# A one-tile first block, Q and K from the unpacked weights, single-row weight loads and five early gate tiles in a fused attention and gMLP kernel

## The chip, the cores and the metric

The kernel runs on one core of a Trainium2 chip. The metric is the device time of one execution in microseconds (us). Before the change it is 280.43 us, the median of three runs (279.98 to 282.6).

## The reference

One block of 2048 tokens with 448 features passes two layers, each with a residual. The first is attention with 16 heads of 28 features over a sliding window of 256 tokens, the second a gMLP: a spatial gating unit whose mixing matrix `w_sp` works over the tokens. A vector `c` gives shift, scale and gate of both.

```python
mod = (_silu(c) @ w_mod).reshape(c.shape[0], 6, 1, -1)
sa, ca, ga, sb, cb, gb = (mod[:, i] for i in range(6))
h = _layernorm(x) * (1 + ca) + sa
x = x + ga * _A_ref(h, A_wqkv, A_wo)
h = _layernorm(x) * (1 + cb) + sb
x = x + gb * _B_ref(h, B_w_in, B_w_sp, B_b_sp, B_w_out)

def _A_ref(x, wqkv, wo):          # H = 16, Dh = 28, W = 256
    q, k, v = split(x @ wqkv)
    scores = q @ k.T * Dh ** -0.5             # 0 <= i - j < W
    return softmax(scores) @ v @ wo

def _B_ref(x, w_in, w_sp, b_sp, w_out):       # Fh = 896
    z = gelu(x @ w_in)
    z1, z2 = z[..., :Fh], _layernorm(z[..., Fh:])
    return (z1 * (w_sp @ z2 + b_sp[:, None])) @ w_out
```

All inputs and the output are bfloat16.

## The kernel before

**Engines and queues.** The tokens are cut into 16 tiles of 128. PE (TensorE) does all matrix products, ACT the exponentials, gelus and some evictions from PSUM, DVE statistics, normalisations and most evictions, POOL the masks, the root of the layer norms and some elementwise work, and SP issues the DMAs (ACT issues two). Every operation is an entry that `P.op` creates, numbered from 0 in the order in which the program creates it. The string `ORDER` lists all entries once. An item such as `125.2/4` is entry 125, done by the third of its possible engines, with slot 4 of its buffer pool. The entries of one engine are emitted in the order of the string, and each engine works its own queue strictly in that order; semaphores make it wait for what other engines deliver. Where entries of different engines stand to each other in the string therefore says nothing; what stands ahead of what on one engine says all.

**The ramp.** SP loads the tokens (`load_x`), two of the six column groups of `w_mod` (`wmodA`, in two halves, the second of them issued by ACT), and the weights of Q, K, V (`wqk_raw`, `wv_sb`). PE runs 44 filler products of 256 columns on zeros (`warm`) and four groups of 16 small ones (`warmt`) between its real work. `c` goes to columns by four one-row products (`c_cols`), ACT takes their silu (`silu0` loads the table, `silu` computes, `exp0` loads the table of the exponential). `modA`, 32 one-column products, gives shift and scale, and two DVE operations evict them (`modAe0`, `modAe1`).

**Blocks.** Tokens are normalised and projected in blocks of 2, 2, 2, 2, 4, 4 tiles (`blocks`). For the first four, `transp_pe` transposes by PE and an eviction to `hT` applies shift and scale; for the last two SP transposes by DMA. The 448 features are held as four chunks of 128 rows, the third of which has 64 rows twice (`CH = (0, 128, 192, 320)`): weights are loaded with these rows doubled, and the doubled half is zeroed (`zv`, `zqk`) or left out. Eight operations (`wqkp`) copy Q and K weights from `wqk_raw` to `WQK`, where each head has 32 columns. `project` runs eight chains of four products per block for Q and K (`qk`), evicted to `QKT` (`qke`), and one chain per tile for V (`v`, evicted by `ve`).

**Attention.** For tile j there are up to three key tiles. `S` is one block of 16 score products, four at a time on strips of 32 rows; two exponentials `E` of 128x1024 follow on ACT, a mask `M` on POOL where needed, and two groups `PV` of eight value products. 90 exponentials are run in all. Then come the division, a DMA transpose (`oT`), the output projection (`wo`), the residual (`x1`), the second layer norm (`l2`, `x2`), a DMA transpose (`h2T`) and shift and scale (`h2m`).

**gMLP.** The gate half `z2` of tile t is seven steps of 448 columns on PE (`z2m`; six full ones and one in which two half-height products run side by side). For ordinary tiles ACT takes the gelu straight from PSUM, which needs a change of the ACT table and so waits for the last exponential. For the raw tiles (`zraw`, tiles 0 and 1) DVE or ACT copies the product to `z2` in SBUF (`z2e`), and ACT takes the gelu from there later. `z1m` and `z1s` give the other half, transposed, in steps of 512 columns. SP transposes `w_sp` in 32 pieces (`wsp`). `G` is 28 groups of 16 products of 512 columns (in quarters), `out` the last product, and `fin` adds the residual.

Of the kernel before, what the change touches and what calls it, by code (L numbers as in the profile page):

```python
# [4 lines left out]
ACT = mybir.ActivationFunctionType  # L5
# [159 lines left out]
0 16 7 1 21 20 17 18 26 23 28 27 118 120 2 3 1673/0 1674 1675 1676 1677 1678 1679 1680 1681 1682 1683 1684 1685 29/2 1686 1687 1688 1689 1690 1691  # L165
1692 1693 1694 25 30 1695 32/1 33 34 31 8 9 14 6 10 5 4 12 15 13 11 50 119 51 121 54 52 122 53 19 22 55 123 24 56 58/0 124 57 125.2/4 126.2/1 35 1696
1697 1698 1699 1700 36 37 1701 60/0 38 1702 1703 39 59/3 127/0 131/2 40 41 49 46 45 48 47.1 128 61 62.1 63.1 65/1 1704 64 1705 1706 132 1707 1708 1709
66 67 134 129.1 130.1 42 43 44 323 319 321 325 324 326 320 322 327 93/3 88/7 98/0 89 90 103/2 104 99 100 101 91 94 83/1 105 68/6 69 106 70 84 102 92
107 133 85 71 78/7 86 79 95 96 80 81 87.1 72 97 73/0 74 82 75 76 113/6 114 115 116 252 185 77 487/0,1 488/3 491/6 328 329 330.1/1 117.1 333.1/4
332.1/3 489 492 331.1/2 1710 108/4 109 110 1711 140/1 111 141 142 1712 1713 143 145/0 146 147 1714 1715 1716 148 502/1,0 112 155/2 156 157 158 186 254  # L170
253 255 187 402 188 189 404 159.1 403 256 144 149 485/1 135/0 136 1717 137 138 1718 165/2 166 167 168 506/0 503/1 486 509/0,1 139 169 493/0 490 170/2
171 1719 1720 172 180/1 181 182 183 173 160/3 161 162 163 510/7 512/9 184 522/0,1 150/1 151 152 153 494 495/1 257 258 507 504 190 408 406 174.1 191
334 336 337 496/1 335 154.1 505/0 513 511 508 407 514 515/2 405 164 526/10 523/3 529/1,2 530/7 192.1/3 193.1/0 259.1/4 175/1 176 177 178 179.1 516/0
533/1 194/0 195 409 196 197 536/0,1 198/1 199 200.1 201.1 222/3 497/2 498 499 500 207/0 223 208 209 210 224 202/1 203 225 539/4 537/5 211 226 549/0,1
553/8 550/6 260.1/1 531 410 501 932 265/2 204 205 206.1 212/3 232/0 213 214 215 233 266 234 235 216.1 517/1 518 519 520 227/3 521 534 524 411 412 554
527 413.1/3 415.1/0 236 268 267 556/1,0 560/0 557/9 228 229 230 538/0 237/2 217/1 525 238 239 231.1 934 218 219 262/3 261 220 240 532 535 340 241.1
221 264.1 263.1 563/1,0 540 528 564/2 566/4 269/1 242/3 314/2 243 270 315 316 317 244 245 576/1,0 541 933 935 542/2 318.1 936 246.1 577/5 580/3 294/0
295 271 272 296 247/2 297 279/3 248 249 280 281 250 273.1 274/1 275 276 282 277 419 543/1 903 900 902 901 298.1 283.1 278.1 251 583/1,0 284/0 299/2
300 301 302 285 286 287 584/7 587/10 303.1 289/1 290 291 292 288.1 590/1,2 591/1 416.1/2 561 558 414.1/1 551 418 339.1 937 341.1 567/0 555 552 938
293.1 939/2 581 578 941/0 588 585 338.1 559 565 562 593/6 603/1,0 544/1 545 546 547 607/8 604/4 568 569/2 548 917/0 918 919 920 921 922 610/2,0 611/9  # L180
923 924 614/2 925 926 309/1 310 311 312 313.1 579/0 589 617/1,2 594 304/1 305 306 586 307 592 582 947 308.1 420 417 612 423.1 605 615 940 570/1 595
596/1 948 906 618/10 620/0 630/1,0 634/5 631/3 347/1 348 349 352/3 571/2 353 354 355 342/0 350 572 637/0,1 573 574 356.1 421 575 351 638/1 641/6 343
344 345 357/1 358 346.1 644/0,2 359 360 621/0 613 616 606 619 645/7 647/2 657/1,0 661/9 658/4 949 950 361.1 951 362/1 635 608 609 622 623/2 632 942
944.1 952 642 953 956.1/2 954.1/1 422.1 639 662 363 387/2 364 388 389 392/3 393 365 372/0 394 366 664/1,0 668/0 665/10 373 390 391.1 669 367/1 368 369
374 370 371.1 395 396.1 424 375 1410 904 1409 597/3 907 598/2 599 1408 624/2 909 943.1 659 957 955 960.1 666 671/0,1 376 674/8 600 601 636/0 377/1 378
379 648 602 672/5 684/1,2 380 685/2 633 640 646 643 688/7 381.1 691/1,0 625/1 626 627 628 649 650/2 629 397/0 398 399 400 401.1 692/1 695/6 698/2,1
382/1 383 384 385 699/3 908 910 905 651/0 911 912 673/0 701/5 660 675 711/0,2 715/4 712/8 386.1 962 964 663 670 667 963 676 677/1 430/1 431 432 433
718/1,2 652/0 653 654 655 434.1 965 966 656 977 978 450/1 451 719/9 722/10 686 693 945.1 689 696 961.1 713 723 716 958.1 720 725/1,0 678/3 914 913
1415 1414 452 714/0 728/0 435/3 436 437 438 729 460/2 453 461 726/8 454 738/1,0 742/0 727 721 739/8 717 724 425/1 426 427 428 462 463 429 745/1,0 967
439.1 968 971/1 969/0 740 730 731/2 749/9 746/10 694/0 690 679/1 680 681 682 464.1 683 979 980 981 982 743 747 750 702 752/2,0 755/4 697 455/1 456 457  # L190
458 687 753/5 765/1,0 700 459.1 703 704/0 445/1 446 447 448 769/1 766/7 772/2,0 773/3 776/6 946.1 732/1 733/0 734 735 736 970 972 1412 1411 705/0 1413
449.1 737 959 983 994 440/1 441 442 779/2,1 782/2 756/0 744 748 741 443 751 780/4 444.1 792/0,1 754 757 758/1 465/1 466 467 468 796/10 799/1,2 793/8
469.1 995 470/0 471 472 473 800/0 986/0 767 777 984/1 770 774 474.1 803/9 480/1 481 482 483 806/0,1 775/0 778 781 771 783 768 484.1 784 785/2 807/5
809/4 819/2,0 823/3 475/1 476 477 478 804 801 794 797 973.1 479.1 987 976 974 808/0 802 798 820/6 826/0,1 810 795 805 830/1 824 821 831 827/2 759/1
915 985 916 828 760/1 761 762 763 811 812/1 833/1,2 764 1007 1008 836/9 825/0 832 927/1 834/5 846/0,2 847/4 850/0 822 837 835 829 853/1,0 929 838
839/0 857/3 854/8 786/3 813/2 1419 1416 840/1 1417 706/3 707 814/2 708 815 816 709 990.1 991.1 988.1 817 860/0,1 975.1 848 858 851 989.1 855 931 930
928 710 818 992 993 996 863/1 861/10 852/0 787/1 788 789 790 849 873/2,1 859 864 856 862 791 997 998 865 866/2 874/2 877/9 875 880/0,2 841/1 842 843
# [22 lines left out]
1585/3 1597/1 1598 1586 1443 1629 1638 1444 1445/1 1446 1568 1455 1456 1570 1621/1 1622 1457/1 1458 1483/3 1541/0 1623 1484 1624 1542 1495/5 1625/1  # L220
1485/0 1496 1487/4 1488 1630 1489/2 1571 1490 1486 1497/3 1615/5 1626 1498 1572 1631/2 1632 1552 1616 1573/0 1617 1574 1618 1619/2 1543/1 1611/6
1599/2 1620 1600 1612 1601/0 1602 1544 1665/5 1666 1657/3 1667/3 1613/2 1668 1658 1669/4 1614 1607/1 1670 1608 1671/0 1659/3 1661/6 1609/2 1603/7 1672
1610 1662 1604 1660 1553/3 1663/0 1554 1664 1491/0 1555/1 1492 1605/2 1556 1606 1493/3 1494
"""

PARAMS = {
# [857 lines left out]
```

## Time and profile before

| quantity | us |
|---|---|
| median of three runs (lowest, highest) | 280.43 (279.98, 282.6) |
| span of the profiled execution, first to last instruction | 279.1 |
| DVE busy in the span | 156.1 |
| ACT busy; of this in 90 exponentials | 135.4; 84.4 |
| POOL busy | 94.2 |
| first modulation product on PE | 8.00 |
| first projection on PE | 11.85 |
| first scores on PE, first exponential on ACT | 17.32, 17.77 |
| last scores on PE | 109.89 |
| granted TensorE clock | 1.000 |

The profile is one execution. A line of the order of time has the start, the time, the engine (PEld is the weight load of PE, ACTq and SPq the DMA queues), the line of the program, the operation, what it writes and reads, how many instructions were merged into it, and in brackets how long the engine had been idle and what ended that. All PE instructions have line 435, so they are told apart by what they write and read. Matmul ends are modelled and overlap the next start, so work is best read from start to start.

### The profile page before, as it was taken

Reading aid. Unit: us, or ns where it says so; the run is one execution under the profiler, and the core shown is the slowest. Engines: PE = TensorE matmul, PEld = TensorE weight load, DVE = VectorE, ACT = ScalarE, POOL = GpSimd, SP = SyncE. Lnnn points to the kernel's source line nnn. Section 1 sums busy time; section 2 is a strip of 40 time slices with the busy share of each in tenths; the row PEclk is TensorE's granted clock in tenths of the full one; section 3 lists DMA queues with packets and bytes.
Section 4 is the critical chain, followed back from the end, with each engine's and each line's share of the span. In section 5 each row is a group of like instructions: output and inputs, shape, how many; then the busy total and the mean of one; then the engine's idle time right before and its main releaser. Section 6 shows DMA issues by size and latency. Waiting matters only on the chain.

```text
span 279.1 us, 6498 instructions
## 1 busy us (share of the span) xinstructions
PE 268.0 (96%) x2750; PEld 142.8 (51%) x2776; DVE 156.1 (56%) x373; ACT 135.4 (49%) x183; POOL 94.2 (34%) x156
## 2 busy tenths in 40 slices
PE   8899999999999988999999999999999999999995
PEld 4667677655565645444344444444444444444452
DVE  5688775576757688597385841332424230433543
ACT  4689999999999999866566600000000000000000
POOL 4166796755568677646322120000000000000000
PEclk9999999999999999999999999999999999999999
DMA  7954129796587683469999700000000000000223
GB/s 240 366 125 76 23 42 203 131 168 161 145 152 133 126 154 77 94 113 169 172 167 189 133 4 0 0 2 0 0 0 0 19 0 0 2 0 0 66 79 105
DMA packets 67503, 25.38 MB, mean 91 GB/s; under 512 B 56337, under 2 KB 67346, under 8 KB 67474
## 3 DMA queue, kind: packets, MB, share of 16 engines
q1 hardware_dynamic: 67200, 24.50, 42.5%
q8 instruction: 22, 0.36, 0.6%
q10 hardware_dynamic: 274, 0.46, 0.5%
q14 instruction: 7, 0.06, 0.1%
HBM read 9.48 MB, written 1.84 MB: 41 GB/s over the span
## 4 chain that ended last, share of the span: by engine, by line
PE 79%; ACT 16%; DMA 2%; issue 1%; DVE 1%; SPq 0%
PE ps L435 79%; ACT PT L796 13%; DMA wmod_sb<-in_w_mod_dram 2%; ACT hT L622 2%; ACT QKT L718 1%; SPq L466 0%; DVE fin L1005 0%; DVE x_sb L842 0%; DVE st_all L543 0%; ACT Vaug L729 0%
## 5 line engine op out<-in xcount | busy, mean ns | idle before, releaser
L796 ACT ACTIVATE PT<-ps 128x1024 bf16<-128x1024 f32 x90 | 84.4, 1078 | 2.6 <-PE ps L435 2.3
L986 DVE TENSOR_TENSOR tmpg<-ps,bsp_bc 128x512 bf16<-128x512 f32 x28 | 19.3, 691 | 59.2 <-PE ps L435 59.2
L435 PE MATMUL ps<-QKT,z 128*128 128x512 bf16 x219 | 50.7, 379 | 0.3
L804 POOL TENSOR_SCALAR_AFFINE_SELECT PT<-PT 128x512 f32<-128x512 f32 x60 | 37.2, 638 | 11.3 <-ACT PT L796 11.3
L435 PE MATMUL ps<-hT,WQK 128*128 128x256 bf16 (+1 forms) x182 | 34.6, 305 | 2.2 <-ACT hT L622 0.8
L435 PEld LDWEIGHTS ps<-QKT,z 128*128 128x128 bf16 x224 | 21.9, 98 | 26.4
L551 POOL TENSOR_TENSOR rs_all<-ve_all,neghalf 128x1 f32<-128x1 f32 (+2 forms) x31 | 20.0, 650 | 38.1 <-DVE ve_all L550 37.8
L435 PE MATMUL ps<-w_in_sb,hT 128*128 128x448 bf16 (+1 forms) x128 | 29.2, 353 | 0.1
L435 PE MATMUL ps<-hT,w_in_sb 128*128 128x512 bf16 (+1 forms) x106 | 27.5, 379 | 0.5 <-DVE st_all L543 0.3
L435 PE MATMUL ps<-w_spC,z 128*128 128x512 bf16 x110 | 26.7, 379 | 0.1
L435 PE MATMUL ps<-w_spD,z 128*128 128x512 bf16 x109 | 26.1, 379 | 0.2
L435 PEld LDWEIGHTS ps<-Vaug,PT 128*128 128x128 bf16 x720 | 22.7, 97 | 5.8 <-ACT PT L796 0.4
L435 PE MATMUL ps<-Vaug,PT 128*128 128x29 bf16 x720 | 25.0, 176 | 0.5 <-POOL PT L804 0.2
L543 DVE BATCH_NORM_STATS2 st_all<-z2raw 128x6 f32<-128x448 bf16 x32 | 18.6, 615 | 10.4 <-ACT z2raw L899 10.3
L435 PEld LDWEIGHTS ps<-hT,WQK 128*128 128x128 bf16 x192 | 16.9, 97 | 10.8 <-ACT hT L622 1.8
L435 PE MATMUL ps<-w_out_sb,z1T 128*128 128x448 bf16 x112 | 22.3, 352 | 0.0
L633 POOL TENSOR_SCALAR hT<-hT,modT 128x256 bf16<-128x256 bf16 (+1 forms) x31 | 18.5, 601 | 10.8 <-DMA hT<-xn 10.8
L564 POOL TENSOR_SCALAR xn<-x_sb,rs_all,nm_all 128x512 bf16<-128x512 bf16 x23 | 17.5, 769 | 8.0 <-DVE nm_all L555 4.3
L543 DVE BATCH_NORM_STATS2 st_all<-x_sb 128x6 f32<-128x448 bf16 x32 | 18.9, 615 | 1.7 <-DMA x_sb<-in_A_x_dram 1.5
L435 PE MATMUL ps<-QKT 28*128 28x128 bf16 x720 | 18.1, 217 | 1.7 <-ACT PT L796 1.3
L721 DVE CAST QKT<-ps 128x256 bf16<-128x256 f32 (+1 forms) x27 | 14.2, 531 | 8.3 <-PE ps L435 7.9
L918 ACT ACTIVATE z1T<-ps 128x512 bf16<-128x512 f32 x28 | 15.6, 600 | 5.8 <-PE ps L435 5.7
(70 smaller groups left out, 273.3 us busy)
## 6 DMA issues: line engine op xcount, KB each, us to landing
wmod_sb<-in_w_mod_dram SPq DMA_DIRECT2D x8, 224.0 KB, 4.0
w_in_sb<-in_B_w_in_dram SPq DMA_DIRECT2D x8, 224.0 KB, 3.8
out_dram<-fin SPq DMA_DIRECT2D x16, 112.0 KB, 1.7
x_sb<-in_A_x_dram SPq DMA_DIRECT2D x3, 448.0 KB, 8.3
wqk_raw<-in_A_wqkv_dram SPq DMA_DIRECT2D x2, 452.0 KB, 7.3
bsp_bc<-in_B_b_sp_dram SPq DMA_DIRECT2D x1, 512.0 KB, 5.8
x_sb<-in_A_x_dram SPq DMA_DIRECT2D x2, 224.0 KB, 3.3
wmod_sb<-in_w_mod_dram ACTq DMA_DIRECT2D x1, 448.0 KB, 4.5
```

Of the source, the lines that this page charges most:

```text
L435: return e.matmul(out_, lhsT=lhsT, rhs=rhs, start=st, stop=sp, **kw)
L543: st = [dve("%sst%d" % (name, i), prio, dve_ns(D), lambda e, i=i, s_=s_: e.bn_stats(st_all[:, slot, t, i, :], s_()), deps, tens) for i, s_ ...
L551: r = pool(name + "rs", prio, 420 + 148 * n, lambda e: e.tensor_tensor(rs_all[:, slot, t0:t1], ve_all[:, slot, t0:t1], neghalf[:, t0:t1], ...
L564: return e.tensor_scalar(dst, src, rs_all[:, slot, t:t + 1], nm_all[:, slot, t:t + 1], ALU.mult, ALU.add)
L622: return e.activation(hT[:, c_, cols], ps[:, ten.slot, q * 256:q * 256 + 256], ACT.Identity, bias=modT[:, c_:c_ + 1], scale=modT[:, 4 + c_ ...
L633: return e.tensor_scalar(hT[:, c_, cols], hT[:, c_, cols], modT[:, base_col + 4 + c_:base_col + 5 + c_], modT[:, base_col + c_:base_col + ...
L718: return e.activation(QKT[:, g, cols], ps[:, ten.slot, 0:w], ACT.Copy)
L721: return e.tensor_copy(QKT[:, g, cols], ps[:, ten.slot, 0:w])
L796: e_op = P.op("E%d_%d" % (j, ui), pr, [("act", 925, lambda e, ten=ten, pt=pt: e.activation(PT[:, pt.slot, :, :], ps[:, ten.slot:ten.slot + ...
L804: ready = pool("M%d_%d" % (j, ui), pr - 50, pool_ns(512), lambda e, pt=pt, pat=pat, cm=cm, cmp=cmp: e.affine_select(out=pt32(pt.slot), in_ ...
L918: g = P.op("z1g%d_%d" % (tb, ft), pr - 19, [("act", act_ns(512), lambda e: e.activation(z1T[:, ft, tb * 512:(tb + 1) * 512], ps[:, ten.slo ...
L986: a = dve("ga%d_%d" % (tb, ft), pr, dve_ns(512), lambda e, tb=tb, ten=ten, tg=tg: e.tensor_tensor(tmpg[:, tg.slot, :], ps[:, ten.slot, :], ...
```

## The change

- `blocks` becomes 1, 1, 2, 2, 2, 4, 4. `transp_pe` has four PSUM banks for the first block and two for the others, and one entry evicts all chunks of a bank.
- The features are held as four chunks of 112 rows. All weight loads become `load_112`, two DMAs of 224 rows; nothing is doubled, and `zv`, `zqk`, `zc`, `cz0` and `cz1` go. wmodA has 16 columns more, wmodG 16 fewer. A memset `xpad` zeroes the pad of `xn`.
- For block 0 Q and K are computed from `wqk_raw`: a step is four products with 32 weight columns each, on four column strips. `WQK` is still packed for the other blocks.
- The scores of tile 0 are two entries of eight products, one for each pair of head groups.
- `zraw` covers tiles 0 to 4. Ordering rules that kept z1, z2, gelus and G behind the last scores or the last exponential are removed from the list of entries.
- `ORDER` is new as a whole. Read per engine, its queues begin, or stand around the end of attention, as follows.

| queue | before | after |
|---|---|---|
| ACT, start | c, wmodA1, silu0, silu, exp0, xn2, xn3 | c, silu0, silu, exp0, wmodA1, xn1 |
| PE, fillers ahead of c_cols | 12 warm, 1 warmt | 19 warm, 3 warmt |
| PE, fillers between modA and the first tr, then up to the first qk | mixed with modA and tr | 5, then 5 behind tr |
| PE, ahead of the first scores | qk of block 0, v of tile 1 | qk of block 0, 28 steps of qk of block 1, two tr of block 2 |
| PE, z steps ahead of the last scores | none | 35 of z2 (tiles 0 to 4), 6 of z1 |
| PE, wo of tiles 14, 15 and last PV | first z steps among them | further back among the z steps |
| SP, w_sp transposes behind the oT of tile 13 | 22 | 28 |

```diff
-    'blocks': (2, 2, 2, 2, 4, 4),
+    'blocks': (1, 1, 2, 2, 2, 4, 4),
+    'raw': (1, 0, 0, 0, 0, 0, 0),
-    'zraw': (0, 1),
+    'zraw': tuple(range(5)),
...
+    def load_112(name, prio, dst, w, a, b, order=(), o=0, engs=("sp", "sp"), rate=292.0):
         return [load("%s%d" % (name, h), prio + 0.001 * h,
-                     lambda e, h=h: e.dma_start(dst[:, 2 * h:2 * h + 2, a - o:b - o], w[192 * h:192 * h + 256, a:b].rearrange("(c p) n -> p c n", p=128)),
-                     256 * (b - a) * 2, order=order, eng=engs[h], rate=rate) for h in range(2)]
+                     lambda e, h=h: e.dma_start(dst[0:R1, 2 * h:2 * h + 2, a - o:b - o], w[224 * h:224 * h + 224, a:b].rearrange("(c p) n -> p c n", p=R1)),
+                     224 * (b - a) * 2, order=order, eng=engs[h], rate=rate) for h in range(2)]
...
-    x0 = load_x("x0", -99, 0, 2)
-    t_wmA = load_dup("wmodA", -98, wmod_sb, w_mod, 0, 2 * D, engs=("sp", "act"), rate=290.0)
+    x0 = load_x("x0", -99, 0, 1)
+    t_wmA = load_112("wmodA", -98, wmod_sb, w_mod, 0, 2 * D + 16, engs=("sp", "act"))
...
+        def raw_chain(g):
+            ten = Ten(B_D if b else B_ALL, guard=True)
+            ops = []
+            for k in range(4):
+                def fn(e, k=k):
+                    last = None
+                    for r in range(4):
+                        a = 112 * g + DH * r
+                        last = mm(e, ps[32 * r:32 * r + 32, ten.slot, 0:w], wqk_raw[0:R1, k, a:a + 32], hT[0:R1, k, cols],
+                                  k == 0, k == 3, tile_position=(0, 32 * r))
+                    return last
...
+                s_ops = []
+                halves = [[Ten(banks((a, a + 1))) for a in a_] for a_ in ((0, 2), (4, 6))] if j == 0 else [tens]
+                for gs, tens in zip(((0, 1), (2, 3)) if j == 0 else ((0, 1, 2, 3),), halves):
+                    deps = [QK_op[(g, blk[j])] for g in gs] + [QK_op[(4 + g, blk[kb])] for g in gs]
+                    s_ops.append(pe("S%d_%d%s" % (j, ui, "h%d" % gs[0] if j == 0 else ""), pr - 50, 270,
+                                    lambda e, j=j, kb=kb, tens=tens, gs=gs: s_mm(e, j, kb, tens, gs), deps, tens, mode=32, order=all_S[-1:]))
...
-                        hst, lambda c_, r: w_in_sb[r, c_, FH + D:FH + 2 * D], D, order=[S_op[(8 if raw else T, 5)]], joint=joint,
+                        hst, lambda c_, r: w_in_sb[r, c_, FH + D:FH + 2 * D], D, joint=joint,
...
-                    evs, [zt], table="gelu", order=[prev_e])
+                         evs, [zt], table="gelu")
```

The two strings begin, with entry 3 the second half of wmodA in both, and silu0, silu, exp0 the entries 25, 30, 31 before and 24, 26, 27 after:

```diff
-0 16 7 1 21 20 17 18 26 23 28 27 118 120 2 3 1673/0 1674 1675 1676 1677 1678 1679 1680 1681 1682 1683 1684 1685 29/2 1686 1687 1688 1689 1690 1691
-1692 1693 1694 25 30 1695 32/1 33 34 31 8 9 14 6 10 5 4 12 15 13 11 50 119 51 121 54 52 122 53 19 22 55 123 24 56 58/0 124 57 125.2/4 126.2/1 35 1696
+16 6 104 159 105 1 46 47 1715/0 1716 1717 1718 0 23 1719 1720 1721 160 1722 1723 1724 1725 1726 1727 1728 1729 1730 1731 1732 1733 18 1734 1735 1736
+17 25/0 24 1737 1738 1739 1740 1741 1742 1743 1744 1745 1746 106 20 107 26 27 1747 1748 1749 2 1750 1751 1752 161 3 28/2 162 29 30 108 48 4 109.2/2
```

## The prediction

> **What bounds the kernel now.** I read the list of engines first, then the order of time of each engine, because a share over the whole span hides that three stages have three limits.
>
> The page's first part, and its chain of waits:
>
> ```profile
> PE 268.0 (96%) x2750; PEld 142.8 (51%) x2776; DVE 156.1 (56%) x373; ACT 135.4 (49%) x183; POOL 94.2 (34%) x156
> PE 79%; ACT 16%; DMA 2%; issue 1%; DVE 1%; SPq 0%
> ```
>
> PE is busy nearly always, so the span is the time at which PE's real work starts, plus that work, plus PE's gaps. Where the gaps are, the order of time shows. The ramp:
>
> ```profile
> 1.35 0.45 ACTq L462 DMA_DIRECT2D wmod_sb<-in_w_mod_dram  x1
> ...
> 4.70 0.26 PE L435 MATMUL ps<-one,crz 1*128 1x1 bf16 x4
> 4.89 0.35 PEld L435 LDWEIGHTS ps<-warm 128*32 128x32 bf16 x16
> ...
> 5.00 0.17 ACT L507 ACTIVATE sc_sb<-ps 128x4 bf16<-128x4 f32 x1 [1.67 <-PE ps L435]
> 5.19 1.28 ACT L509 ACT_TABLE_LOAD   x1
> ...
> 8.00 0.55 PE L435 MATMUL ps<-sc_sb,wmod_sb 128*128 128x1 bf16 x16 [0.73 <-DMA wmod_sb<-in_w_mod_dram]
> ...
> 11.85 2.09 PE L435 MATMUL ps<-hT,WQK 128*128 128x256 bf16 x14
> ...
> 17.32 0.40 PE L435 MATMUL ps<-QKT 28*128 28x128 bf16 x16
> ```
>
> The modulation (8.00) waits for the load of w_mod; the first projection follows at 11.85, the first scores at 17.32. Then comes attention, in the order of time of ACT:
>
> ```profile
> 83.35 12.96 ACT L796 ACTIVATE PT<-ps 128x1024 bf16<-128x1024 f32 x14
> 99.62 4.93 ACT L796 ACTIVATE PT<-ps 128x1024 bf16<-128x1024 f32 x5
> 105.06 7.44 ACT L796 ACTIVATE PT<-ps 128x1024 bf16<-128x1024 f32 x8 [0.51 <-PE ps L435]
> ```
>
> Exponentials run back to back at 0.92 us each (12.96 / 14) to 112.5, and the last scores start at 109.89. So attention is paced by ACT and PE together. A piece of PE's list ends some 0.16 us after the next could start, so I take 0.16 off each piece; the gaps left are some 1 us in 10 to 15 us, some 17 us from 17.3 to 110, and under 3 us from 110 to the end. After 110 PE is full; only PE work that goes, or moves into those 17 us, can help.
>
> **Prices of PE instructions**, start to start: 512 columns 0.219 us (49 in 10.74), 448 columns 0.19 (4 in 0.92 less 0.16), 256 columns 0.11, a block of scores 0.335, eight value products 0.21 (48 in 1.36).
>
> **The ramp.** Orders are per engine, so I read the new order string as one queue for each. Two things move. On PE the four c-column products stand behind nine more filler groups; the time from 4.89 to the end of those fillers before is 2.1 us, so they start near 6.9 in place of 4.70. On ACT the second half of wmodA, formerly issued at 1.35, now stands behind silu0, silu and exp0. Silu follows the columns by 0.30, and silu to the end of exp0 takes 1.70 (5.00 to 6.70, with the table load of 1.28): the issue starts at 8.9. Its landing has no row at this time. Lower end: 0.45 issue, 0.7 as for the load of c, and 408 KB at the 366 GB/s of the second slice, two thirds of it while SP's loads share the engines: 1.7; sum 11.8. Upper end: the list of DMA issues gives 4.5 us from issue to landing for this very load, 13.4. I take 12.3, near the lower end since the SP queue has then only 1.5 of its 4.2 MB left. The modulation starts 4.3 us later. It has no filler inside it now (16 loads in 0.47 us, so 32 in 0.95): done at 13.3, evicted by 13.7. Fillers and one-tile transposes (five at 0.11, then 0.45) and the first hT eviction (about 0.45) put the first raw projection at 15.15, against 11.85.
>
> From there to the first scores the queue of PE has 32 raw steps of four 32-column matmuls and 28 steps of 128 columns. The row of 16 such small weight loads (0.35) gives 0.0875 a step, 2.8 us; a 128-column step is 0.058 at half the 256-column price, 1.6 us. Before, this stretch held 32 of 0.11 and one value chain, in 5.5 us. DVE now has, from its modulation copies to its first eviction of block 1, seven hT pieces (0.4 each, estimated from 0.53 for twice the columns), two packs (0.29), four evictions (0.3) and a statistic (0.8 with its aggregate): 5.4 us, from 13.9 to 19.3, and a bank for the last QK groups waits for that eviction. Those groups and the evictions of ACT behind them (0.2 each) take 1.4 more. Scores start at 20.7, **3.4 us later** (bounds 2 and 5). Splitting the first scores in halves does not bring them earlier, as block 1 is queued ahead of both halves. The smaller loads (408 for 458 KB) save under 0.3 us each and lie under the late one. Dropped c copies and zero fills were off the path: nothing. If the late load were hidden, the ramp would be 0.9 us shorter than before instead.
>
> **Work moved out of the last stage.** Before, no z2 or z1 step stands ahead of the last scores on PE. In the new order five whole gate tiles do (35 steps at 0.19, 6.7) and six z1 steps (0.22 each, 1.3): 8.0. Two value groups that stood ahead of them now stand behind, 0.4 back. **7.6 us less** is left behind the last scores. Eleven fillers that ran in attention (1.2 us) are gone; that is in the next sum.
>
> **What attention pays for it.** From first scores to those of tile 12, PE has 68.4 us of work by the prices against 67.3, ACT 67.5 against 69.0 (66 exponentials in both): I hold the 71.7 us of before. From there to the last scores (20.9 us before) PE had 17.0 and ACT 20.2; now PE has 23.0 and ACT 22.1 (three z2 evictions and one value eviction more, 0.45 each). By ACT alone at the fill of before (20.2 / 20.9) this takes 22.9; by PE at 94%, the fill of the busiest stretch (tiles 1 to 8: 43.0 of work in 45.8), 24.4. Middle 23.7: **2.8 us more**, bounds 0 (all goes into gaps) and 5.
>
> **The last stage.** The raw tiles' extra DVE copies (seven of 0.62) lie in attention, where DVE has a third of its time free; uncovered, 4.3 us. The last value products stand 11.0 us behind the last scores on PE, formerly 3.9, so oT15, the layer norm of tiles 14, 15 and h2T14 come that much later. From the last output projection (15.7) add 0.8 for the residual, 0.8 statistics, 0.9 variance and root, 0.8 normalisation, two transposes on SP (1.3 each, 2.8 to landing), 1.0 modulation: 24.5 to 26. z2 of tile 14 is due at 25.5, formerly at 31.7. Also 27 w_sp transposes are queued behind the last scores on SP, formerly 21, and 19 of them and the bias load behind h2T14, which issues at some 22.5. At 1.3 us each (13 of them between 142 and 159) and 2.5 to landing, wsp0_3, the seventh, lands at 34 for a G matmul due at 38, and wsp1_3, the thirteenth item, at 42 for one due at 43. **1.5 us of stalls**, bounds 0 and 6.
>
> **Sum:** 3.4 + 2.8 - 7.6 + 1.5 = +0.1 us. On the profiled run's span of 279.1 that is 279.2. The three times have a median of 280.43; what lies around the span and between runs is 1.3. I predict 280.5 us, no change.
>
> **Rivals.**
> - *The fill is free.* ACT sets the pace to the end and z work uses gaps only: 3.4 + 0 - 7.6 + 0.4 gives -3.8, so 276.6. For it: the gaps of 0.51 and 0.52 us in front of PE at 102 to 108 wait for ACT; against it: 94% is all PE reached elsewhere. A late load that lands at 11 would add another 1.3. Chance 0.32.
> - *The layer norm of tiles 14 and 15 arrives late.* If DVE, which is busy for 9.68 of the 10 us from 120 to 130, puts 3 to 4 us between the links of that chain, PE stands in front of z2 of tile 14 for it, and the transposes behind h2T14 come that much later too: +3.7, 284.2. It decides once the chain is over 1 us longer than the 24.5 summed. Chance 0.16.
> - *PE slows down after its wait.* The ten first fillers took 1.84 us of weight loads, 0.18 each, where later ones take 0.11: PE starts at a slower pace. Its fillers now end near 9.4 and the modulation starts at 12.3, a hole of 2.9 us; the longest in the ramp before was 0.7. If the slow pace returns for some 3 us, raw steps take up to twice as long: +2.8, so 283.3. Chance 0.10, as the hole of 0.7 shows nothing of it and the granted clock is 9 tenths or more in all slices. The Trainium skill, in TensorE: Matmul & The Clock Gate, under "What's actually happening", says that the array falls back to half its clock after an idle window of some 3.4 us. By that rule the case would come in only if the load lands after some 12.8; no run here has such a hole.
> - *The changed start does not happen:* the late load is not late. Then the ramp is 0.9 shorter instead of 3.4 longer, and the sum -4.2, 276.2; it is in the 0.32.
>
> **How the numbers follow.** A difference of 1% is about what a measurement here can tell. No change, 277.6 to 283.2, has 0.42; faster 0.32; slower 0.26 (the two rivals). The likeliest case alone reaches 277.8 to 283.2. For eight in ten I take in the free fill and the late chain: 275.3 to 285.5.
>
> **What would show it.** The ACT-queue issue of wmod_sb at about 8.9 and the modulation at 12.3; first scores near 20.7; last scores near 116 with 35 z2 steps ahead of them; first matmul on w_sp 37 us behind them. If the modulation starts before 10, the ramp is wrong; if the last scores come before 114, the fill was free; a wait of PE on hT above 2 us behind 135 is the second rival.

## The result and the profile after

The changed kernel takes 294.97 us (median of 4 runs, 291.67 to 295.48) against 281.44 us (279.98 to 282.6) of the kernel before on the same chip: ratio 1.047, 95% interval 1.040 to 1.054. It is slower, by 13.5 us, where no change was forecast. The profiled execution took 295.48 us, its span is 293.8 us against 279.1: 14.7 us more. Two profiles below, a_load and a_zlate, are of executions over 1.5% above the fastest of their kernel, so what waits for what is read from them, and not how long the whole takes.

Three marks cut the span: first scores, last scores, end.

| stage | before | after | measured | forecast |
|---|---|---|---|---|
| start to first scores | 17.32 | 25.62 | +8.3 | +3.4 |
| first scores to last scores | 92.57 | 105.44 | +12.9 | +2.8 |
| of it, from the scores of tile 12 on | 20.9 | 25.7 | +4.8 | +2.8 |
| last scores to end | 169.2 | 162.7 | -6.5 | -6.1 |

The page of the changed kernel: busy time of the engines, PE's granted clock in the 40 slices, and the chain that ended last.

```profile
PE 273.1 (93%) x2880; PEld 143.5 (49%) x2896; DVE 166.5 (57%) x394; ACT 133.3 (45%) x179; POOL 93.3 (32%) x154
...
PEclk9969999979999999999999999999999999999999
...
PE 69%; DMA 7%; ACT 7%; DVE 6%; SPq 6%; POOL 2%; issue 1%; POOLq 0%
```

PE's share of the chain fell from 79% to 69%; DMA and SP's queue, 2% together before, have 13%. Two slices of the clock are under 9, where before none was.

The start, in the order of time of ACT, then of PE (columns as in the prediction):

```profile
7.61 0.17 ACT L488 ACTIVATE sc_sb<-ps 112x4 bf16<-112x4 f32 x1 [4.75 <-PE ps L439]
7.80 1.28 ACT L490 ACT_TABLE_LOAD   x1
7.82 0.35 ACTq L447 DMA_DIRECT2D wmod_sb<-in_w_mod_dram  x1
```

```profile
16.40 0.99 PE L439 MATMUL ps<-sc_sb,wmod_sb 112*128 112x1 bf16 x32 [6.64 <-DMA wmod_sb<-in_w_mod_dram]
...
20.33 1.80 PE L439 MATMUL ps<-hT,wqk_raw 112*32 112x128 bf16 x112
...
25.62 0.29 PE L439 MATMUL ps<-QKT 28*128 28x128 bf16 x8
...
27.54 0.32 PE L439 MATMUL ps<-ident,xn 128*112 128x128 bf16 x2 [1.12 <-ACT PT L829]
```

The second half of wmodA leaves ACT's queue at 7.82 and PE waits 6.64 us for it. The chain in order of time says the same in one line, and the list of DMA issues from 0 to 18 us has the sizes (of one) and the median times from issue to landing:

```profile
7.82 8.45 DMA wmod_sb<-in_w_mod_dram
```

```profile
wmod_sb<-in_w_mod_dram ACTq DMA_DIRECT2D x1, 399.0 KB, 8.4
wo_sb<-in_A_wo_dram SPq DMA_DIRECT2D x2, 196.0 KB, 10.1
```

Loads of 196 KB take 10 us, too, so the time is not that of moving a load's own bytes. What each queue moved (q1 is SP's, q10 ACT's; packets, MB, share of the 16 engines) says more, first from 7.8 to 11 us, then from 12 to 14:

```profile
q1 hardware_dynamic: 1018, 0.99, 107.7%
```

```profile
q10 hardware_dynamic: 219, 0.38, 64.7%
q1 hardware_dynamic: 247, 0.21, 38.8%
```

For 3 us and more behind its issue nothing of the late load moved; once it moved, it had the larger part. At 7.82 SP's queue had issued 3.4 MB and moved 1.5. From there to the landing at 16.27 both queues moved 2.5 MB, 0.30 a us; at that rate the 1.9 MB in flight and the load's own 0.4 take 7.8 us, an estimate near the 8.45. The order of landing is near the order of issue, but not quite: the load landed behind one issued at 5.26 and just ahead of three that SP had issued at 6.05, 6.55 and 7.06 (landings 16.5, 17.1, 17.8). Before, the same half left at 1.35 with 4.5 us to landing.

PE's clock behind that wait, in windows (length; busy time and number of instructions of PE, its weight loads, DVE, ACT, POOL; granted clock; DMA share; GB/s):

```profile
15.00:20.00 5.00, 3.60 (x50) 3.11 (x50) 1.77 (x8) 0.84 (x2) 1.83 (x3) 0.50 0.80 205
20.00:25.00 5.00, 3.90 (x144) 3.29 (x143) 4.82 (x13) 2.69 (x10) 2.57 (x3) 0.95 0.01 3
```

The last part of attention, in the order of time of ACT:

```profile
108.49 9.27 ACT L829 ACTIVATE PT<-ps 128x1024 bf16<-128x1024 f32 x10
117.82 0.54 ACT L923 ACTIVATE z<-ps 128x448 bf16<-128x448 f32 x1
118.36 1.94 ACT L829 ACTIVATE PT<-ps 128x1024 bf16<-128x1024 f32 x2
120.26 0.54 ACT L923 ACTIVATE z<-ps 128x448 bf16<-128x448 f32 x1
120.80 1.94 ACT L829 ACTIVATE PT<-ps 128x1024 bf16<-128x1024 f32 x2
...
125.88 1.94 ACT L829 ACTIVATE PT<-ps 128x1024 bf16<-128x1024 f32 x2 [0.55 <-PE ps L439]
128.51 1.94 ACT L829 ACTIVATE PT<-ps 128x1024 bf16<-128x1024 f32 x2 [0.69 <-PE ps L439]
131.51 1.94 ACT L829 ACTIVATE PT<-ps 128x1024 bf16<-128x1024 f32 x2 [1.06 <-PE ps L439]
```

Before, the exponentials ran back to back up to 112.5, with one break of 0.51 us. Now from 117.8 they come two and two, and between the pairs ACT copies a gate tile or stands for PE. The reason is in the picks of the order string: from the third group of scores of tile 13 on, scores use two pairs of banks in turn, the third pair is lent to the gate tiles, so a group of scores waits for both exponentials of the group ahead.

Between 28 us and the last scores PE has two waits of over 0.6 us, in its order of time:

```profile
53.49 0.92 PE L439 MATMUL ps<-wo_sb,oT 112*128 112x448 bf16 x4 [1.64 <-DVE mv_all L527]
...
59.62 0.94 PE L439 MATMUL ps<-sc_sb,wmod_sb 112*128 112x1 bf16 x32 [1.17 <-DMA wmod_sb<-in_w_mod_dram]
```

The first ends 0.1 us behind the landing of an attention output (53.4), which SP's queue had issued at 50.88 behind transposes of tokens, so it is put down to that and not to DVE. The clock is 0.66 from 60 to 65.

Behind attention only one stall of PE is over 0.6 us, and it is for a transpose of w_sp:

```profile
177.18 3.19 PE L439 MATMUL ps<-QKT,z 128*128 128x512 bf16 x14 [1.34 <-DMA QKT<-in_B_w_sp_dram]
```

### The profile page after: what moved, and what is told of

It is laid out like the page before. It is cut to its first block, busy times and chain, and to the rows that moved or that the text cites. A ratio compares the mean times of both kernels' runs of the same rounds, so it can differ in the third digit from the quotient of the medians.

```text
span 293.8 us, 6768 instructions
## 1 busy us (share of the span) xinstructions
PE 273.1 (93%) x2880; PEld 143.5 (49%) x2896; DVE 166.5 (57%) x394; ACT 133.3 (45%) x179; POOL 93.3 (32%) x154
## 4 chain that ended last, share of the span: by engine, by line
PE 69%; DMA 7%; ACT 7%; DVE 6%; SPq 6%; POOL 2%; issue 1%; POOLq 0%
PE ps L439 69%; ACT PT L829 5%; SPq L988 5%; DMA wmod_sb<-in_w_mod_dram 4%; DMA QKT<-in_B_w_sp_dram 2%; DVE st_all L524 2%; POOL PT L835 1%; DMA hT<-xn 1%; POOL rs_all L532 1%; ACT z1T L949 1%; DVE wo_sb L779 1%; DVE QKT L736 1%; DVE WQK L652 1%; POOL hT L628 1%; DVE mv_all L527 0%
## 5 line engine op out<-in xcount | busy, mean ns | idle before, releaser
L829 ACT ACTIVATE PT<-ps 128x1024 bf16<-128x1024 f32 x90 | 85.5, 1039 | 11.2 <-PE ps L439 10.9
L439 PE MATMUL ps<-hT,WQK 112*128 112x256 bf16 (+2 forms) x192 | 35.3, 309 | 1.2 <-DVE QKT L736 1.1
L439 PE MATMUL ps<-w_in_sb,hT 128*128 128x448 bf16 (+1 forms) x128 | 27.9, 353 | 0.4 <-POOL hT L628 0.2
L439 PEld LDWEIGHTS ps<-Vaug,PT 128*128 128x128 bf16 x720 | 23.5, 97 | 7.8 <-DVE o_sb L860 0.9
L439 PE MATMUL ps<-w_spC,z 128*128 128x512 bf16 x109 | 25.6, 379 | 0.1
L628 POOL TENSOR_SCALAR hT<-hT,modT 128x256 bf16<-128x256 bf16 (+1 forms) x28 | 17.0, 611 | 15.6 <-DMA hT<-xn 15.5
L439 PEld LDWEIGHTS ps<-hT,WQK 112*128 112x128 bf16 x192 | 16.0, 100 | 9.7 <-DVE QKT L736 1.6
L736 DVE CAST QKT<-ps 128x256 bf16<-128x256 f32 (+2 forms) x33 | 16.4, 505 | 5.5 <-PE ps L439 5.2
L439 PE MATMUL ps<-wo_sb,oT 112*128 112x448 bf16 x64 | 16.6, 354 | 2.7 <-DVE mv_all L527 1.6
L545 POOL TENSOR_SCALAR xn<-x_sb,rs_all,nm_all 128x512 bf16<-128x512 bf16 (+1 forms) x21 | 15.9, 761 | 8.8 <-DMA hT<-xn 5.7
```

Source lines behind the costliest of these rows:

```text
L439: return e.matmul(out_, lhsT=lhsT, rhs=rhs, start=st, stop=sp, **kw)
L545: return e.tensor_scalar(dst, src, rs_all[:, slot, t:t + 1], nm_all[:, slot, t:t + 1], ALU.mult, ALU.add)
L628: return e.tensor_scalar(hT[:, c_, cols], hT[:, c_, cols], modT[:, base_col + 4 + c_:base_col + 5 + c_], modT[:, base_col + c_:base_col + ...
L736: return e.tensor_copy(QKT[:, g, cols], ps[:, ten.slot, 0:w])
L829: e_op = P.op("E%d_%d" % (j, ui), pr, [("act", 925, lambda e, e_in=e_in, e_out=e_out: e.activation(e_out(), e_in(), ACT.Exp, scale=SCALE)) ...
```

## The experiments

Edits of the order are given as queues of one engine. Each time is compared with runs of the kernel before on the same chip (medians 280.4 to 281.4).

### The late load alone, undone and done

In the changed kernel the load goes back behind c:

```diff
 ACT queue (a_load)
-c silu0 silu exp0 wmodA1 xn1
+c wmodA1 silu0 silu exp0 xn1
```

> The changed kernel with one entry moved: the ACT queue issues the second half of wmodA right behind the load of c, ahead of silu0, silu and exp0. Theory (the late load costs the whole ramp): the modulation starts near 9.6, when PE is through its fillers, instead of 16.4; first scores at 17 to 18 instead of 25.6; the granted clock of 0.50 between 15 and 20 us is gone; if nothing later moves, 294.97 - 8 = 287 (285 to 289). Rival (attention waits for something that comes at a time of its own, the w_mod loads that land at 57 to 59): the stall ahead of modB grows by what the ramp gains, and the time falls by 4 or less, 291 or more.

Measured: 286.56 us (285.79 to 291.21), ratio 1.0185 (1.0147 to 1.0223), 8.4 us under the changed kernel, as the theory has it. Modulation at 8.52, first scores at 18.69. Two points of the theory failed: the clock is still half in the start (0.50 from 14.5 to 17.5 and from 21.5 to 24.5), and the first scores are 0.7 late. A single execution doesn't place them well: in a_load_modb, a_sp, a_zlate and a_z3, which start as a_load does, they stand at 16.91, 18.19, 17.73 and 17.06. The same move, done to the kernel before:

```diff
 ACT queue (b_late)
-c wmodA1 silu0 silu exp0 xn2
+c silu0 silu exp0 wmodA1 xn2
```

> The kernel before with one load moved: the ACT queue issues the second half of wmodA behind silu0, silu and exp0, at about 5.2 us instead of 1.35. Theory (the DMA engines serve loads in the order of issue whatever queue they come from): it lands behind the token load that SP issues at 3.5, at 12.5 to 13.5 instead of 5.9, the modulation starts then, and the time grows by 4.5 to 6 us, 285.5 to 287.5. Rival (the ACT queue keeps a share of its own, as its 4.5 us from issue to landing before suggests): it lands at 9.7 and the time grows by 1.5 to 2.

Measured: 287.34 us (286.14 to 289.26), ratio 1.0208 (1.0157 to 1.0259). The chain has the load issued at 5.21 and landing 6.38 us later:

```profile
5.21 6.38 DMA wmod_sb<-in_w_mod_dram
11.72 2.51 PE ps L435 x42
```

So a move of one issue costs 5.9 us before and 8.4 us after. The time is as the theory has it, the landing at 11.6 lies between theory (12.5 to 13.5) and rival (9.7), and it is 0.2 us ahead of that of the tokens that SP issued at 3.34 (11.8): strict order of issue does not hold here either. Two issue times, 5.21 and 7.82, give 6.38 and 8.45 us.

### The clock in the start

The late load stays late, and PE is given work of no effect while it waits:

```diff
-    for i in range(44):
+    for i in range(102):
 PE queue (a_warm)
+58 fillers ahead of modA
```

> The changed kernel with 58 more fillers of 256 columns (0.11 us each, 6.4 us) in PE's queue ahead of the modulation, where PE stood idle for 6.8 us waiting for the late half of wmodA. Nothing else is changed: the late load stays late. Theory A (the idle stretch takes PE's clock down, and the half clock of 15 to 20 us costs time): the granted clock stays above 0.9 in 15 to 20, the first raw projection comes within 4.0 us of the modulation as before, the first scores at 23 to 24.3 instead of 25.62, the whole 1.5 to 2.5 us under the changed kernel: 292.5 to 293.5, ratio to before 1.038 to 1.042. Theory B (the stretch is slow because DVE and ACT release its operands late; the clock is a bystander): the clock is full there, but first scores stay at 25.3 or later and the time at 294.5 or more.

The order of time of PE:

```profile
16.88 0.94 PE L441 MATMUL ps<-sc_sb,wmod_sb 112*128 112x1 bf16 x32 [0.97 <-DMA wmod_sb<-in_w_mod_dram]
...
19.31 1.99 PE L441 MATMUL ps<-hT,wqk_raw 112*32 112x128 bf16 x112
...
23.81 0.29 PE L441 MATMUL ps<-QKT 28*128 28x128 bf16 x8
```

From the modulation to the first scores it is 6.93 us in place of 9.22, and the clock is 1.00 from 10 to 25: in this stretch theory A holds, the half clock cost 2.3 us. The whole missed its band and did not gain: 296.28 us (292.71 to 297.33), ratio 1.0495 (1.0397 to 1.0593). The 1.8 us won at the first scores had grown to 4.9 at those of tile 12 (100.48 against 105.35) and were lost at 110 us, where the profile shows a wait that the changed kernel had not, on DVE and then on PE:

```profile
111.11 0.58 DVE L538 SCALAR_TENSOR_TENSOR nm_all<-mv_all,rs_all 128x2 f32<-128x2 f32 x1 [2.57 <-POOL rs_all L534]
```

```profile
112.95 1.67 PE L441 MATMUL ps<-wo_sb,oT 112*128 112x448 bf16 x4 [2.30 <-DVE x_sb L875]
```

DVE waits for a root from POOL; the residual sum queued behind it holds a bank that PE wants; and PE runs at half clock from 112 to 119. The next kernel takes that wait away too (on SP's queue a w_sp transpose also goes ahead of the one of tile 6):

```diff
 DVE queue (a_warm2)
-x1_10 l2_6nm x2_6 x1_8 rec12 nrm12 x1_11
+x1_10 x1_8 rec12 nrm12 l2_6nm x2_6 x1_11
```

> The kernel a_warm (changed kernel with 58 more fillers in the idle stretch of the ramp) with a normalisation of tile 6 (its mean times root, and the normalised tile) moved behind the residual sums of tile 8 and the value division of tile 12 on DVE. In a_warm DVE waited 2.57 us for the root on the way, the residual sum of tile 8 behind it held a bank, PE stood 2.46 us, and its clock was half for the next 7 us. Theory A continued (the 1.8 us won in the ramp was given back there): no such wait at 110, full clock from 112 to 120, the time 2 to 5 us under the 296.28 of a_warm: 291.3 to 294.3, that is 1 to 3 under the changed kernel. Rival (the wait comes up elsewhere): within 1 us of a_warm.

Measured: 292.05 us (290.01 to 292.65), ratio 1.034 (1.0263 to 1.0418), as theory A has it: 4.2 us under a_warm and 2.9 under the changed kernel. Its clock was full but for the last 0.4 us of the span. The interval overlaps those of a_warm and of the changed kernel a little; in the profiled spans, 293.8 and 290.6, the difference is 3.2 us.

### Waits in attention: they move

In a_load PE waited 1.59 us up to 47.80 and 1.54 us up to 54.30, for an attention output and for w_mod of the second modulation, both behind transposes that were waiting on SP's queue. First the loads were moved ahead, then an attention output too:

```diff
 SP queue (a_load_modb)
-hx10 hx8 hx9 oT2 wmod3_1 wmod4_1 hx11 wmod3_0 wmod4_0 oT3
+wmod3_1 wmod4_1 wmod3_0 wmod4_0 hx10 hx8 hx9 oT2 hx11 oT3
 SP queue (a_sp, from a_load_modb)
-hx10 hx8 hx9 oT2 hx11
+hx10 oT2 hx8 hx9 hx11
```

> As a_load, and the four loads of the w_mod groups for modB stand on SP ahead of the DMA transposes hx10, hx8, hx9, oT2, hx11 instead of behind them. Theory (PE's two gaps of 1.8 and 1.3 us at 51.7 and 58.3, and the granted clock of 0.83 from 60 to 70, come from modB waiting in PE's queue for those loads): both gaps and the slow stretch go, 3 to 5 us less than a_load, 282 to 284. Rival (PE has other work missing there, and the gaps only move): within 1.5 us of a_load.

Measured: 288.74 us (288.45 to 289.76), ratio 1.0278 (1.0243 to 1.0314). That is 2.2 us over a_load, outside both forecasts: with the loads ahead the kernel is slower, and the intervals don't overlap. The wait for w_mod is gone, one of 2.05 us for an attention output ends at 46.56, one of 1.33 for another at 57.78, and the half clock stands at 46 to 50 in place of 55 to 59.

> The changed kernel with wmodA's second half issued behind c, the four loads of w_mod of the second modulation ahead of the transpose of tile 10 on SP's queue, and the transpose of attention output 2 moved ahead of those of tiles 8 and 9. Theory E (SP's queue, which serves in order, holds back that transpose; PE then waits 2.2 us in front of its output projection, and its clock falls for the next 4 us): the wait at 44 to 47 us is under 0.5 us, the clock stays full in 46 to 50, the time 2 to 3.5 us under the 288.74 of the same kernel without this move: 285.3 to 286.7. Theory F (such waits only change place, because attention as a whole has a fixed sum of PE work and waits): the last scores start at 123.5 to 124.5 as there, the time 288 to 289.5.

Measured: 288.45 us (288.23 to 289.02), ratio 1.0262 (1.0205 to 1.0319): a miss of theory E, as theory F has it. The wait ahead of 46.56 is gone, waits of 0.86 and 0.95 us ahead of value products have come, up to 49.80 and 53.62, the half clock stands at 52 to 59. Last scores are at 124.05, in a_load_modb at 123.97.

### First scores whole

```diff
-                halves = [[Ten(banks((a, a + 1))) for a in a_] for a_ in ((0, 2), (4, 6))] if j == 0 else [tens]
-                for gs, tens in zip(((0, 1), (2, 3)) if j == 0 else ((0, 1, 2, 3),), halves):
+                halves = [tens]
+                for gs, tens in zip(((0, 1, 2, 3),), halves):
```

> The changed kernel with wmodA's second half issued behind c and with the first scores whole, as before, in two pairs of banks instead of halves in four. Theory G (the halves hold all eight banks, so that PE stands 1.29 us until the first exponential is done, and the clock falls in 20 to 25): no gap over 0.5 us between the first scores and the transposes of block 2, second group of scores of tile 1 some 1 us earlier against the first scores, the clock full in 20 to 25, the time 1 to 3 us under the 286.56 of the kernel that has only the early load: 283.5 to 285.5. Theory H (the wait is covered later by what attention waits for anyway): the same 286.56 within 0.7 us. Whole scores start the first exponential some 0.4 us later; that is in both.

Measured: 286.74 us (285.73 to 289.14), ratio 1.0227 (1.0147 to 1.0306), against 286.56 of a_load: theory H in the time. The places did change: first scores 16.93, no wait of PE over 0.9 us around the first exponential, clock full from 14 to 25; but waits of 1.71 us up to 44.44 and of 0.91 up to 50.30 remain, with half clock at 52 to 56.

### Gate tiles out of attention, without and with the third pair of banks

From a_load_modb the 35 z2 steps, their copies and six z1 steps were moved behind the last scores; the scores kept two pairs. Three of the gate copies then stand ahead of the last two exponentials on ACT.

> As a_load_modb, with the 35 z2 steps of tiles 0 to 4, their ten evictions and the six z1 steps moved from ahead of the last scores to right behind them. Theory (the z work fills gaps of PE in attention, which grew by about 5 us from tile 12 on for 8 us of work taken in): the last scores come 4 to 5 us earlier than in a_load_modb, 8 us more stand behind them, and the time is 2 to 4 us longer. Rival (the fill is what stretches attention, so it gains nothing): the same time or less than a_load_modb.

Measured: 301.49 us (298.39 to 303.46), ratio 1.0689 (1.061 to 1.0767): 12.8 us over a_load_modb, outside both forecasts. The last scores are 2.4 us later (126.42), not 4 to 5 earlier. PE, without that work:

```profile
112.99 0.61 PE L439 MATMUL ps<-QKT 28*128 28x128 bf16 x16 [2.28 <-ACT PT L829]
115.65 0.61 PE L439 MATMUL ps<-QKT 28*128 28x128 bf16 x16 [2.05 <-ACT PT L829]
```

Each group of scores waits for both exponentials ahead, and the scores themselves take 0.61 in place of 0.40: the clock is half from 112 to 122. With the third pair given back, and the last two exponentials put ahead of the gate copies:

```diff
 picks of the pairs (a_z3): S14_0 S14_2 S14_4 S15_0 S15_2 S15_4
-0,1 0,1 0,1 0,1 1,0 0,1
+2,1 0,1 2,0 1,2 0,1 2,0
```

> The kernel a_zlate (changed kernel, w_mod loads early, gate tiles and z1 steps moved behind the last scores) with the third pair of banks given back to the scores from the third group of tile 13 on, and with the last two exponentials ahead of the gate copies on ACT. Theory C (banks set the pace there): exponentials back to back, tile 12 to the last scores 20.5 to 22 us, no half clock between 110 and 125, the time 8 to 12 us under the 301.49 of a_zlate: 289.5 to 293.5. Rival (the new order of projections and values keeps that stretch slow without gate tiles): tile 12 to the last scores 25 us or more, 298 to 301.

Measured: 301.9 us (301.2 to 304.65), ratio 1.0724 (1.0621 to 1.0826): a miss of theory C, near the rival's band. Sixteen exponentials ran back to back from 99.75 to 114.5, as theory C has it, but PE, with little to do between the scores, fell to half clock from 111 to 121, and from then on it was late for ACT; tile 12 to the last scores took 24.85 us. So in the changed kernel, whose clock is full from 65 on, the work in the gaps also keeps PE's clock up there.

### The banks alone

The kernel before, no work moved, two pairs of banks for the last seven groups of scores:

```diff
 picks of the pairs (b_banks): S13_4 S14_0 S15_0 S15_2 S15_4
-1,2 0,2 2,1 0,2 1,2
+1,0 0,1 0,1 0,1 0,1
```

> The kernel before with one thing of the change: the last seven groups of scores (from the third of tile 13 to the third of tile 15) use two pairs of PSUM banks in turn and not three, as the new order has them because its gate tiles hold the third pair. No work is moved. Theory C (the banks set the pace: scores wait for both exponentials of the group ahead, so ACT stands some 0.5 us after each pair): exponentials in the last stretch of attention come in pairs with a gap of about 0.5 us ahead of each, tile 12 to the last scores 23.5 to 24.5 us instead of 20.9, the whole 2.5 to 4 us slower than before: ratio 1.009 to 1.014. Theory D (PE's added 8 us of work is what slows this stretch, the banks are no limit): the exponentials stay back to back, the time within 0.5 us of before.

Measured: 289.1 us (287.65 to 289.85), ratio 1.0276 (1.0212 to 1.034). The order of time of ACT, then windows:

```profile
99.27 1.94 ACT L796 ACTIVATE PT<-ps 128x1024 bf16<-128x1024 f32 x2 [0.51 <-PE ps L435]
101.78 1.94 ACT L796 ACTIVATE PT<-ps 128x1024 bf16<-128x1024 f32 x2 [0.57 <-PE ps L435]
104.44 1.94 ACT L796 ACTIVATE PT<-ps 128x1024 bf16<-128x1024 f32 x2 [0.72 <-PE ps L435]
108.08 1.94 ACT L796 ACTIVATE PT<-ps 128x1024 bf16<-128x1024 f32 x2 [1.70 <-PE ps L435]
```

```profile
101.00:106.00 5.00, 3.67 (x69) 2.24 (x70) 3.83 (x6) 3.71 (x5) 1.74 (x4) 0.55 0.78 128
...
116.00:121.00 5.00, 3.96 (x10) 0.99 (x8) 1.38 (x7) 2.75 (x3) 2.54 (x5) 0.50 0.26 54
```

The pairs with a gap are those of the changed kernel, so theory C holds for the mechanism; the size, 8.7 us, is over twice its upper figure, and the clock fell as well. To price the two apart, seven fillers were put ahead of six of the groups:

```diff
+    for g in range(6):
+        l_ten = Ten(banks((5,)))
+        for i in range(7):
+            pe("late%d_%d" % (g, i), 1000, 110, lambda e, l_ten=l_ten: mm(e, ps[:, l_ten.slot, 0:256], warm[:, 0:128], warm[:, 0:256], True, True), [t_warm], [l_ten])
```

> The kernel b_banks (before, with two pairs of banks for the last seven groups of scores) with seven fillers of 256 columns (0.77 us) on PE ahead of six of these groups, in a bank that nothing else uses there. They take the place of PE's idle time, not of its work. Theory C with the clock as a second part: the granted clock stays full from 96 to 122; the exponentials still come in pairs with some 0.5 us ahead of each; last scores 3.5 to 4.5 us later than before and not 5.1; the time 3 to 5 us under the 289.1 of b_banks: 284.1 to 286.1, ratio to before 1.013 to 1.020. Rival (banks alone, the clock only goes along): the fillers bring nothing, 288 to 290.

```profile
101.00:106.00 5.00, 4.19 (x88) 2.65 (x91) 3.97 (x7) 3.88 (x4) 2.01 (x4) 1.00 0.84 126
...
116.00:121.00 5.00, 5.00 (x56) 2.37 (x54) 1.28 (x4) 2.08 (x4) 1.86 (x4) 1.00 0.37 30
```

Measured: 286.7 us (285.76 to 287.73), ratio 1.021 (1.0164 to 1.0255). All seven pairs have 0.51 to 0.55 us ahead of them, and between the third group of tile 13 and the last scores it is 14.72 us, before 11.70. The profiled spans split the loss: before 279.1, with full clock 284.1, without fillers 287.8, so 5.0 us are the banks and 3.7 the clock. The medians, against before on the same chip, split it otherwise: 6.2 and 2.4, and the intervals of the two ratios overlap a little. The fillers stand in PE's queue, so what they cost themselves is counted with the banks. The time came 0.6 us above the expected band.

### Filling gaps without the third pair

The kernel before, with gate tiles 0 and 1 in the banks that scores do not use:

```diff
 PE queue (b_fill2)
-S13_4 PV13_1 PV13_3 gateB S14_0 ... S14_4 PV14_1 wo11 PV14_0 S15_0
+S13_4 z2m0 S14_0 PV13_1 PV13_3 PV13_0 PV13_5 gateB ... S14_4 z2m1 S15_0 PV14 wo11
```

> The kernel before with gate tiles 0 and 1 (14 steps of z2, 2.7 us of PE) moved from behind the last scores into tiles 13 to 15, in the two banks that scores do not use, evicted by DVE; the scores keep their three pairs of banks. Theory I (attention ends late only where the third pair is missing; PE has gaps of 3.9 us from tile 12 to the last scores): exponentials stay back to back but for 0.5 us at one or two places, last scores 0.5 to 1.5 us later than before, 2.7 us of work less behind them, the whole 1 to 2 us faster: ratio 0.993 to 0.997. Theory J (any work put between the scores costs attention its full length or more): last scores 3 us or more later, the time as before or up to 2 us slower.

Measured: 284.06 us (283.12 to 286.84, 10 runs), ratio 1.0104 (1.0061 to 1.0148). Theory J in the last scores, and not I; the time is 3.4 us over before (median 280.68), above both bands. The clock was full throughout, yet the last scores came 4.6 us later for 2.7 us of moved work. The first gate tile moved the next scores by 0.2 us only; then value products waited for its eviction (0.39), the second tile for a bank that DVE was reading (0.69), an output projection for a residual sum (1.76). The last of these is in part of the edit's own making: on DVE it also set that residual sum, of tile 11, behind a normalisation that waits for a root from POOL (0.81) and a division, where before it stood ahead of them. What the fill cost came from what is queued behind it; how much a better place for that sum would save was not tried.

### All together

a_nohalf with the SP moves of a_sp and the DVE and w_sp moves of a_warm2.

> The changed kernel with wmodA's second half issued behind c, first scores whole, loads of w_mod for the second modulation and the transpose of attention output 2 early on SP, and the normalisation of tile 6 late on DVE. If the parts add up: 294.97 less 8.4 (early load) less some 2 to 3 (clock) gives 283.5 to 284.6, and what is left over before, 3 to 4 us, is the attention stage, S0 to the last scores 102 to 104 us against 92.6, less the 6.5 of the last stage. If they overlap (a wait taken away comes up at the next place, and the clock falls there): 286 to 289, as the parts taken one by one.

Measured: 285.55 us (284.19 to 288.15), ratio 1.0182 (1.0109 to 1.0255), between the two expected bands. Span 283.9: first scores 18.07 (+0.75 against before), first to last scores 103.8 (+11.2), the rest 162.0 (-7.2). Only 3.4 us within attention were at half clock. The ratio is that of a_load, 1.0185: of the moves it joins, only the early load shows a gain clear of the intervals. None of the variants beat the kernel before.

## Why the prediction was wrong

**Where the ramp failed.** The prediction had the issue at 8.9, behind the table load. It came at 7.82, beside it. The step that failed is the landing, 3.4 us from issue where 8.45 were measured: "I take 12.3, near the lower end since the SP queue has then only 1.5 of its 4.2 MB left". What counted was not what SP had still to issue but what it had issued and not landed, 1.9 MB. Landing was at 16.3, beyond the upper bound of 13.4, which came from a load issued at 1.35 with hardly anything ahead of it. a_load and b_late show this term, together with the clock that falls in the wait (0.50 from 10 to 16.5 in b_late, too). By the Trainium skill, DMA: Bandwidth & Descriptors, section Queues, rings and completion order, each DMA engine takes turns between queues packet by packet. The trace agrees for the time in which the load moved, 0.38 MB beside 0.21 of SP's from 12 to 14 us. The 3 us and more before, in which nothing of it moved, do not follow from this rule, and their cause stays open.

**The work behind it** was not costed too short: 8.4 us from modulation to first scores, 6.93 at full clock in a_warm, where the other inputs had long been ready, and 8.2 in a_nohalf with the early load. "If the late load were hidden, the ramp would be 0.9 us shorter" is not shown: a_nohalf and a_all, with the same start, have first scores 0.4 us earlier and 0.75 later than before.

**The clock** was the rival with a chance of 0.10, "PE slows down after its wait", and it happened: "if the load lands after some 12.8" was its condition. It cost 2.3 us in the ramp. The idle stretch of 6.6 us agrees with the Trainium skill's rule that the prediction cited. What the prediction did not see is that the clock falls in attention too: in b_banks at 101.5, with no gap of PE over 0.86 us in the 10 us ahead of it. The same page, TensorE: Matmul & The Clock Gate, section A second HAM failure mode: psum-queue depth-cycling, tells of that: short idle times between groups that wait for PSUM make the clock swing. The runs agree, 0.55 from 101 to 106 in b_banks and 1.00 with those places filled.

**Attention up to tile 12** was held at 71.7 and took 79.7. The step that failed is the comparison of sums over twelve tiles: by the queues of the kernel the sums are right to some 1 us, their places were not, and the term had no bound. Tiles 4 and 5 took 17.25 us against 11.59, with waits of 1.64 and 1.17 us of PE and a clock of 0.66 from 60 to 65; in a_warm2, without these and at full clock, 13.51. Tile 11 took 7.95 against 5.32, as 7.2 us of PE work by the prices stand there and 4.8 before. From first scores to those of tile 1 it was 4.03 against 2.84, with the wait for the first exponential, as the halves hold all eight banks. The remaining tiles lie within 1.4 us of before, in both directions. The prediction had seen waits for banks in the ramp, but put no price on SP's queue, where transposes of tokens waited 3.0 and 2.0 us ahead of an attention output and of the loads of the second modulation. That this queue is the cause of the loss is not shown: a_load_modb and a_sp took these waits away one after the other and gained nothing, and a_warm lost them by its start alone. With full clock and no wait of PE over 0.61 us from tile 1 to tile 12, a_warm2 still takes 76.1 us up to tile 12; these 4.4 us over the forecast, 1.1 of them work, are not explained.

**From tile 12 on** the term was 2.8 with bounds 0 and 5; it measured 4.8. The mechanism was wrong, though inside its bounds: it asked whether PE or ACT has more work, 23.0 and 22.1, while neither sets the pace. A group of scores and its two exponentials follow each other without overlap, 2.45 us a pair instead of 1.85, because the third pair of banks is lent out. b_banks shows that with no work moved. That the term came out inside its bounds is luck. How much of the 4.8 is the banks in the changed kernel itself is not measured: there the gate copies fill ACT's gaps, and a_z3 lost the clock.

**The last stage** was right: -7.6 of moved work and +1.5 of stalls made -6.1, measured -6.5. The stall is for w_sp behind the layer norm of tile 14 and 15, 1.34 us at 177; the first w_sp matmul came 39.3 us behind the last scores, forecast 37. The second rival, a late layer norm in front of PE, did not come: no wait of PE on hT behind 135.

**The range**, 275.3 to 285.5, missed 294.97: the ramp alone exceeded its bound of 5 by 3.3, and attention up to tile 12 had no bound.

What stays open: a_all has nearly all long waits and half clocks taken away and still spends 11.2 us more between first and last scores. 7.1 of that is PE work by the prices of the prediction, moved there from behind; the other 4 were not taken apart. A new order of the projections alone was not tried.

## What to carry to other kernels

A load that was issued late landed, here, near its turn among all loads of both queues: cost it by the bytes in flight at its issue, not by the bytes that are still to be issued. Work moved into gaps needs more than time in the gap: list the banks it takes and what then waits for them, and follow the instructions queued behind its eviction. Compare work per tile, not per stage, and check that what is taken out of PE does not leave it so idle that its clock falls.

## What the runs showed of the hardware

A DMA issue on ACT's queue went out at 7.82, 0.02 us behind the start of a table load of 1.28 us, not behind its end. A load on ACT's queue, issued at 7.82 with 1.9 MB of SP's in flight, moved nothing up to 11 us and landed at 16.27. PE's clock fell to half in stretches of some 3.4, 7 or 10 us, also without a long gap: in b_banks PE was busy for 1.90 of the 3.4 us from 98.1 and the clock was 0.50 in the next 3.4, while with fillers, 3.29 of 3.4 busy, it stayed at 1.00. The busy share alone does not decide: b_fill2 had 1.64 of 3.4 us from 110.8, and its clock stayed at 1.00. Fillers, work of no effect, kept the clock up there; the medians are 286.7 us for b_banks_warm and 289.1 for b_banks.
